# Fused attention and MLP on one core: scores and products in 64x32 tiles

## The chip, the core and the metric

The kernel runs on one core of a Trainium2 chip. A core has engines with a queue each: TensorE (PE; its weight loads are listed as PEld), VectorE (DVE), ScalarE (ACT), GpSimd (POOL) and SyncE (SP), which here only issues DMAs. Each engine takes its instructions in order; they wait for each other by semaphores. The metric is device microseconds (us) of one execution. Three runs of the kernel before took 413.98, 414.71 and 415.77 us.

## The reference

```python
def reference(A_x, A_wqkv, A_wo, B_x, B_w1, B_b1, B_w2, B_b2):
    # _A_ref: x @ wqkv -> 16 heads of 28; softmax(q k^T * 28**-0.5) v; @ wo
    # _B_ref: gelu(x @ w1 + b1, tanh form) @ w2 + b2
    x = A_x                                  # 1 x 2048 x 448, bfloat16
    xn = _layernorm(x, axis=-1)
    s = _A_ref(xn, A_wqkv, A_wo)
    g = _silu(_B_ref(xn, B_w1, B_b1, B_w2, B_b2))   # hidden width 1792
    return x + s * g
```

So there is a softmax over 16 heads x 2048 x 2048 scores, an MLP with 448 x 1792 and 1792 x 448 weights, and projections of 448 x 448.

## The kernel before

*Tiling.* A head's 28 elements are padded to 32, so that four heads fill 128 partitions: four head groups g. The queries are cut into four chunks c of 512. A block b = 4g + c holds the work of one head group on one chunk: 16 tiles of 128 keys x 4 heads, 64 score tiles m of 128 keys x 512 queries, each one PSUM bank. There are 16 blocks and 1024 score tiles. (In the last block, the tiles are cut to 256 and then to 128 queries, so that the end can begin earlier.) The eight PSUM banks are one pool, `ring`, which all matmuls share.

*The chain for a score tile.* TensorE writes the scores into a bank (`t_score`, L1731). Then either ScalarE takes the exponential of two or three neighbouring banks in one instruction (`p_exps`, L1785), or VectorE makes an approximate exponential of one bank by integer arithmetic (`p_apass`, L2065) for tiles set apart ("late", by fours, one for each head, `p_late`); for the late tiles, VectorE (L2138) or POOL (L2132) then writes two shifted copies, which are multiplied with scaled values `vs`. TensorE multiplies the results with the values (`t_pv`, L2320) and adds up over the keys in one accumulator bank per block. A 1 in the padded values gives the softmax denominators too.

*The other products.* Projections q, k, v, the hidden layer (`p_f1`), the second layer (`p_f2`) and the output projection (`p_out`) go through `_mm` (L128), in the same queue between the scores. Gelu of the hidden layer is done at one stretch on ScalarE (L1620), since it needs another function table; tanh for silu comes in four instructions (L1657, L1692). Block b ends in `p_epi`: VectorE copies the accumulator (L2404) or adds it to a partial sum kept in SBUF (L2210, L2212, L2402), the denominators go by DMA through DRAM and POOL's power (L2416) and return as `rb`, and POOL multiplies (L2427) into the place of the block's queries. An output tile of 128 rows needs the four blocks of its chunk; `t_oev` multiplies it with the gate and adds x, by ScalarE's copy and VectorE (L2454, L2456, L2465, L2479) where all exponentials are out, by VectorE (L2458) otherwise.

*Tile shapes of TensorE.* A matmul can use a part of the 128 x 128 array, given as rows x columns. Three shapes are used: 128x128 at the start, 128x32 for all products (four side by side, one for each 32 columns of the output), 32x128 for scores (each head's 32 rows; up to four heads side by side, each into its own bank). `four` lets a score task take four banks; `rest`/`finish` split the last, half empty k tile of a product into two 32x128 matmuls that join a score task; `p_pad` and `p_alone` put one head's queries into `qpad`, zeros for the other heads, so that a single late score tile can run in shape 128x32.

*Order of the work.* The order of all instructions is fixed at build time by a planner (`run`). It keeps a modelled time for each engine, and takes the task that can start first, weighted by priorities and due marks (`planned`). `start_of` gives a task's start: in its terms a change of shape costs `SWITCH` and scores of different heads overlap. `put` issues the task with the waits that it needs. `BP` is a table of constants for each block (`tune`); `NQ` gives the number of late quads in each block, `BN` bursts with partial sums.

Of the kernel before, what the change touches and what calls it, by code (L numbers as in the profile page):

```python
# [16 lines left out]
DH = 28  # L17
F = 1792
G = 4
# [6 lines left out]
NP = 18  # L26
# [4 lines left out]
BPN = ('S4', 'QF', 'MG', 'GQ', 'GE', 'EPS', 'HP', 'JIT', 'RM', 'RG', 'WT', 'PV0', 'PVC', 'MP', 'ND4', 'LU', 'JOINT', 'LQ', 'JMAX', 'DQ', 'URG', 'SLACK', 'UR', 'QLEAD', 'QDIST', 'R3', 'CN', 'CS', 'SR', 'PS', 'PQ', 'BN', 'PVB')  # L31
BP = (
# [17 lines left out]
)  # L50
NQ = (14, 4, 4, 4, 7, 14, 7, 16, 8, 15, 5, 9, 6, 8, 12, 8)
# [45 lines left out]
SEM, OWN, SEMW = 0.07, 0.03, 0.15  # L97
SWITCH = 0.1
# [16 lines left out]
class _Buf:  # L115
    __slots__ = ("w", "r", "tw", "tr")

    def __init__(self):
        self.w = None
        self.r = []  # L120
        self.tw = None
        self.tr = 0.0


def _mm(eng, out, w, x, start, stop):
    ins = None
    for q in range(0, 128, 32):
        ins = eng.matmul(out[q:q + 32, :], w[:, q:q + 32], x, tile_position=(0, q), start=start, stop=stop, skip_group_check=True)  # L128
    return ins


class _Task:
# [6 lines left out]
    def __init__(self, E, fn, reads=(), writes=(), dur=0.1, lat=0.05, prio=5, w=1.0, mode="col", rows=(), port=False, tx=False):  # L139
        self.E, self.fn, self.reads, self.writes = E, fn, list(reads), list(writes)  # L140
        self.dur, self.lat, self.rank, self.w = dur, lat, prio, w
        self.mode, self.rows, self.port, self.tx = mode, set(rows), port, tx
        if E == DVE:
            ov = min(OVERLAP, 0.4 * self.dur)
            self.dur, self.lat = self.dur - ov, self.lat + ov


class _Kernel:
    def __init__(self, nc, A_x, A_wqkv, A_wo, B_w1, B_b1, B_w2, B_b2, out):
# [11 lines left out]
        self.rest_toks = {}  # L161
# [10 lines left out]
        self.run_toks = set()  # L172
# [34 lines left out]
    def start_of(self, t):  # L207
        s = self.tE[t.E]
        if t.E == PE and t.mode != self.pe_mode:
            s += SWITCH  # L210
        elif t.E == PE and t.mode == "row" and not (t.rows & self.pe_rows):
            s = self.pe_start + 0.01
# [9 lines left out]
        for b in t.writes:  # L222
            mine = b.w is not None and b.w[0] is own
            if not (t.E == PE and mine):
                s = max(s, (b.tw or 0.0) + (OWN if mine else SEM))
            s = max(s, b.tr + (SEMW if t.mode == "row" and t.E == PE else SEM))
        return s

    def put(self, t, start=None):
        if start is None:  # L230
            start = self.start_of(t)
        self.deps(t.E, t.reads, t.writes)
        if t.port and t.E == POOL and start < self.port[POOL] + 4.0:
            self.wait(POOL, self.port_h)
# [8 lines left out]
        if t.E == PE and t.mode == "row":  # L243
            for b in map(id, t.writes):
                if self.rest_toks.get(b) is not None:
                    self.wait(PE, self.rest_toks.pop(b))
                elif b in self.rest_toks:
                    self.rest_toks[b] = (sem, self.evcnt[PE])
        self.prog[t.E].append(lambda eng, f=t.fn, s=sem: f(eng).then_inc(s, by))
        h = (sem, self.evcnt[key])  # L250
        if t.E == PE:
            if t.mode == self.pe_mode == "row" and not (t.rows & self.pe_rows):
                self.pe_rows |= t.rows
            else:
                self.pe_rows = set(t.rows)
            sw = SWITCH if t.mode != self.pe_mode else 0.0
            if t.mode != self.pe_mode:
                self.run_toks = set()
            self.run_toks |= set(map(id, t.writes))
            self.pe_mode, self.pe_start = t.mode, start  # L260
            self.pe_hist.append((start - sw, start + t.dur * t.w))
# [4 lines left out]
        self.tE[t.E] = max(self.tE[t.E], start + t.dur)  # L266
# [6 lines left out]
        if self.after and t.E == PE and t.mode == "row":  # L273
# [89 lines left out]
    def choose(self):  # L363
# [7 lines left out]
        b = self.next_m // 64  # L371
        if self.four(at):
            return True
# [12 lines left out]
        return True  # L386

    def four(self, at):
        p, t, m = self.pend, self.pend["task"], self.next_m
        if not S4 or len(at) < 4 or len(p["ms"]) < 2 or not 64 <= m < MTOT - 2 or self.gu is None and m >= GM - 6 or self.in_gelu():  # L390
            return False
        n = m + 1
        while n in self.late:
            n += 1
        if n >= MTOT or {self.pieces(x)[1] for x in p["ms"]} & {self.pieces(m)[1], self.pieces(n)[1]}:
            return False
        lim = self.start_of(t)
        if lim is None or not self.can(m, lim) or not self.can(n, lim) or QF and self.lq and self.can(self.lq[0][0], lim):
            return False
        lim += JOINT  # L400
        if S4 > 2:
            lim = max(lim, p["due"]() - RM)
        fr = {i: f for i, f in at.items() if f <= lim}
        if len(fr) < 4 or len(fr) - 4 - self.over() < (1, 0, 1, 0, -9)[S4 - 1]:
            return False
        two = [x + y for x in self.runs(fr, 2) for y in self.runs(fr, 2) if x[1] < y[0]]
        if not two:
            return False
        t.writes = [self.b_ring[i] for i in min(two, key=lambda y: max(fr[i] for i in y))]
        return True  # L410
# [23 lines left out]
    def run(self):  # L434
        idle = 0
        while True:
# [5 lines left out]
            for p in self.procs:  # L442
# [11 lines left out]
                elif x[0] == "banks" and x[1]():  # L454
                    ids = self.first(self.idle(), p[3][3])
                    if ids:
                        t = _Task(PE, None, (), [self.b_ring[i] for i in ids], 0.216, 0.17, p[3][2])
                        cand.append((self.start_of(t), p, t))
                elif p[3][0] == "bank" and free is not None and p[5]() and p[3][1]():
                    t = _Task(PE, None, (), [self.banks[free][1]], 0.216, 0.17, *p[3][2:])  # L460
# [19 lines left out]
            if E == PE and t.prio >= UR:  # L480
                sc = [c for c in cand if c[2].E == PE and c[2].prio == 1 and c[2].mode == "row"]
# [2089 lines left out]
```

## Time and profile before

| | |
|---|---|
| runs | 413.98, 414.71, 415.77 us (median 414.71) |
| span of the profiled execution | 412.4 us (its first to its last instruction) |
| mean granted TensorE clock | 1.000 |
| TensorE busy | 395.3 us, 6157 matmuls |
| TensorE weight loads | 144.0 us, 6157 |
| ScalarE busy | 400.7 us, 409 instructions |
| VectorE busy | 345.6 us, 596 |
| POOL busy | 194.7 us, 221 |

The profile has no time of its own around the span; the runs' median is 2.3 us above the span. Busy time counts the pipelined overlap of neighbours on an engine, so the distance between starts tells more about an engine's load than the sum of its durations. In the timeline's lines stand the start, the time of the group, engine, line, operation, output and input by the program's names, sizes, the count, and in brackets the idle time before and what ended it. `xnT`, `h`, `w`, `x_sb`, `kT`, `vaug` appear as targets of exponentials, because their space is used again once they have been read.

### The profile page before, as it was taken

The page shows a single profiled execution, that of the slowest core. Times are in us where ns is not written, and L with a number is a line of the kernel's source. Part 1 is how long each engine was busy: PE and PEld are TensorE (multiplying, and loading weights), DVE is VectorE, ACT ScalarE, POOL GpSimd, SP SyncE. Part 2 cuts the span into 40 slices and gives each one's busy share as a digit, 9 for nine tenths or more (in the row PEclk, how much of TensorE's full clock was granted, in tenths as well). Part 3 has the DMA queues.
Part 4 walks back from the last instruction along what each step waited for, and adds up shares of the span by engine and source line. Part 5 has one row for each costly group of instructions (what it writes and reads, how often), then busy time and mean ns, then how long its engine had stood idle before and what let it go on. Part 6 is the DMA issues. An engine that isn't in the chain of part 4 may idle for free.

```text
span 412.4 us, 14687 instructions
## 1 busy us (share of the span) xinstructions
PE 395.3 (96%) x6157; PEld 144.0 (35%) x6157; DVE 345.6 (84%) x596; ACT 400.7 (97%) x409; POOL 194.7 (47%) x221
## 2 busy tenths in 40 slices
PE   6999999999999999999999999999999999999996
PEld 5543232333322233232224443332332223333453
DVE  8958798896679888989898117999998999899976
ACT  6999999999999999999999999999999999999995
POOL 7494656649982563255632411156157014553040
PEclk9999999999999999999999999999999999999999
DMA  8801110001000000100330000220010003200072
GB/s 254 288 4 42 4 31 2 23 12 30 18 3 30 2 28 8 33 2 2 99 105 18 28 3 7 53 54 12 21 24 10 27 8 58 72 3 29 24 140 94
DMA packets 18784, 17.56 MB, mean 43 GB/s; under 512 B 8941, under 2 KB 15421, under 8 KB 18686
## 3 DMA queue, kind: packets, MB, share of 16 engines
q1 hardware_dynamic: 16734, 13.55, 11.1%
q0 software_dynamic: 1008, 2.49, 3.5%
q8 instruction: 49, 0.80, 0.8%
q10 hardware_dynamic: 976, 0.57, 0.5%
q14 instruction: 17, 0.14, 0.1%
HBM read 12.54 MB, written 2.88 MB: 37 GB/s over the span
## 4 chain that ended last, share of the span: by engine, by line
PE 65%; ACT 20%; issue 8%; DVE 5%; POOL 1%; ACTq 0%; DVEq 0%; POOLq 0%
PE ring L128 31%; PE ring L1731 17%; PE ring L2320 14%; ACT P L1785 12%; ACT h L1785 7%; ACT xnT L1785 2%; PE ring L1293 1%; PE ring L1544 1%; DVE x_sb L2065 1%; DVE st L1036 1%; PE ring L1142 1%; DVE h L2065 0%; PE ring L1109 0%; PE ring L1224 0%; POOL h L1095 0%
## 5 line engine op out<-in xcount | busy, mean ns | idle before, releaser
L1785 ACT ACTIVATE P<-ring 128x1024 bf16<-128x1024 f32 (+1 forms) x236 | 249.3, 1162 | 1.1 <-PE ring L2320 0.3
L1731 PE MATMUL ring<-qT,kT 32*128 32x512 bf16 (+2 forms) x1131 | 130.5, 359 | 5.3 <-ACT P L1785 1.6
L1785 ACT ACTIVATE h<-ring 128x1024 bf16<-128x1024 f32 (+1 forms) x79 | 85.8, 1177 | 0.4 <-PE ring L2320 0.3
L1731 PEld LDWEIGHTS ring<-qT,kT 32*128 32x128 bf16 x1131 | 35.6, 91 | 119.9 <-ACT P L1785 60.2
L2065 DVE TENSOR_SCALAR vaug<-ring 128x512 uint16<-128x512 f32 x92 | 61.0, 683 | 5.9 <-PE ring L1731 3.8
L128 PE MATMUL ring<-xnT,w 128*32 128x512 bf16 x864 | 57.6, 381 | 0.4 <-ACT h L1785 0.2
L128 PE MATMUL ring<-w,h 128*32 128x448 bf16 x896 | 55.5, 355 | 0.2 <-DVE x_sb L2065 0.2
L2320 PE MATMUL ring<-P,vaug 128*32 128x512 bf16 (+2 forms) x606 | 53.7, 351 | 0.8 <-ACT xnT L1785 0.7
L2427 POOL TENSOR_TENSOR qT<-x_sb,E_sb 128x512 bf16<-128x512 f32 x15 | 17.7, 1179 | 67.3 <-PE ring L1731 19.0
L2416 POOL TENSOR_TENSOR rc<-rs,mone 128x16 f32<-128x16 bf16 x11 | 32.7, 2971 | 29.5 <-DMA rs<-E_sb 27.9
L1785 ACT ACTIVATE xnT<-ring 128x1024 bf16<-128x1024 f32 (+1 forms) x39 | 43.1, 1132 | 0.6 <-PE ring L1731 0.6
L2065 DVE TENSOR_SCALAR w<-ring 128x512 uint16<-128x512 f32 x52 | 34.6, 685 | 2.7 <-PE ring L1731 2.1
L128 PEld LDWEIGHTS ring<-xnT,w 128*32 128x32 bf16 x864 | 20.3, 96 | 26.3 <-issue 6.1
L128 PEld LDWEIGHTS ring<-w,h 128*32 128x32 bf16 x896 | 17.9, 95 | 22.8 <-issue 14.0
L2320 PE MATMUL ring<-h,vaug 128*32 128x512 bf16 x201 | 23.4, 383 | 0.4 <-ACT P L1785 0.4
L1435 DVE CAST qT<-ring 128x512 bf16<-128x512 f32 x15 | 10.3, 688 | 15.3 <-PE ring L128 15.0
L2065 DVE TENSOR_SCALAR h<-ring 128x512 uint16<-128x512 f32 x28 | 18.7, 684 | 3.8 <-PE ring L1731 3.6
L2320 PEld LDWEIGHTS ring<-P,vaug 128*32 128x32 bf16 x606 | 15.9, 95 | 15.5 <-issue 7.2
L1558 DVE CAST h<-ring 128x512 bf16<-128x512 f32 x24 | 16.4, 687 | 5.0 <-PE ring L128 4.9
L2065 DVE TENSOR_SCALAR x_sb<-ring 128x512 uint16<-128x512 f32 x28 | 18.5, 682 | 2.5 <-PE ring L1731 1.6
L1441 POOL TENSOR_TENSOR qsq<-qT 128x512 bf16<-128x512 bf16 x12 | 12.5, 1039 | 15.5 <-DVE qT L1435 15.5
L128 PE MATMUL ring<-wv,xnT 128*32 128x112 bf16 (+1 forms) x512 | 18.1, 261 | 0.5 <-issue 0.3
(248 smaller groups left out, 644.0 us busy)
## 6 DMA issues: line engine op xcount, KB each, us to landing
x_sb<-recs SPq DMA_DIRECT2D x60, 64.0 KB, 2.0
w<-in_B_w_dram SPq DMA_DIRECT2D x1, 1568.0 KB, 7.5
w<-in_B_w_dram SPq DMA_DIRECT2D x1, 1344.0 KB, 8.3
x_sb<-in_A_x_dram SPq DMA_DIRECT2D x2, 448.0 KB, 6.8
out_dram<-in_A_x_dram SPq DMA_DIRECT2D x2, 448.0 KB, 10.6
out_dram<-h POOLq DMA_DIRECT2D x4, 224.0 KB, 5.9
out_dram<-h SPq DMA_DIRECT2D x7, 112.0 KB, 2.7
xnT<-wq POOLq DMA_DIRECT2D x1, 512.0 KB, 5.4
```

Of the source, the lines that this page charges most:

```text
L128: ins = eng.matmul(out[q:q + 32, :], w[:, q:q + 32], x, tile_position=(0, q), start=start, stop=stop, skip_group_check=True)
L1036: yield _Task(DVE, lambda eng, i=i, t=t: eng.bn_stats(K.st6[:, i, :], K.x_sb[:, c, t, :]), [K.b_x1t if i == 4 else K.b_x[c] if c else K.b_ ...
L1142: return eng.matmul(bank, w[sl, 3, g * 128:(g + 1) * 128], K.xnT[sl, 3, c * 512:(c + 1) * 512], tile_position=pos, start=False, stop=True, ...
L1435: yield _Task(DVE, lambda eng: eng.tensor_copy(qb, bank), [tok], [qr], 0.7, 0.0, dp)
L1441: yield _Task(POOL, lambda eng: eng.tensor_tensor(qs, qb, qb, ALU.mult), [qr], [tq], 1.1, 0.05, 2, port=True)
L1558: yield _Task(DVE, lambda eng: eng.tensor_copy(dst, bank), [tok], wr, 0.69, 0.0, 2)
L1731: return eng.matmul(dst, K.kT[32 * j:32 * j + 32, g, t * 128:(t + 1) * 128], K.qT[32 * j:32 * j + 32, g, c * 512 + q0:c * 512 + q0 + nq], ...
L1785: return eng.activation(reg[:, i0:i0 + n, :], src, ACTF.Exp, scale=SM_SCALE)
L2065: yield _Task(DVE, lambda eng: eng.tensor_scalar(K.part(u, k).bitcast(dt.uint16), K.like(u, bank), SM_SCALE * LOG2E * 128.0, (127.0 - EXP_ ...
L2320: return eng.matmul(acc[32 * j:32 * j + 32, q0:q0 + nq], w, ap[:, col:col + nq] if len(ap.shape) == 2 else ap[:, col // 128:(col + nq) // ...
L2416: yield _Task(POOL, lambda eng: eng.tensor_tensor(K.rc[:, :], K.rs[:, :], K.mone[:, 0:1].to_broadcast([128, 16]), ALU.pow), [K.b_srs, K.b_ ...
L2427: yield _Task(POOL, lambda eng: eng.tensor_tensor(dst, K.rb, E, ALU.mult), [K.b_rb, tE], [K.b_onT[g][c]], 1.15, 0.05, 1, port=True)
```

## The change

Block 0 and the last block stay in the shapes of before. From the point where the padded queries of block 0 have landed, to the end of block 14, scores and products are matmuls of 64x32: four columns of tiles and two halves of rows, h = 0 and 1.

- *Scores* (`t_half`). A half's 64 rows hold two heads. `qp` holds the queries of one head in 32 of the 64 rows and zeros in the other 32, so the matmul over 64 rows gives one head's scores. There are two such arrangements (v) and two buffers (blocks by turns). `p_strips` fills them by four DMAs on SP for each block, 60 in all, ahead of the block; POOL clears them once (two memsets). `JM` changes the order of the heads, so that neighbouring score tiles are on different halves. A tile needs four matmuls of 64x32 for its four key strips.
- *Products* (`product`, `t_pv`). Each k tile of 128 is run as two halves, first all k tiles on one half, then on the other. Both add to the same bank. Where a bank goes from one half to the other with nothing read between, `put` adds a wait of TensorE on its own semaphore ("turn"). The empty half of the last k tile is left out. Two products may be under way at once (`PW`).
- *Planner.* It keeps a time for each half (`tH`), and a constant each for issue, step and turn.
- *Removed*: `rest`, `finish`, `four`, `p_alone`, `qpad`. `P` has 16 slots in place of 18; `qst` shares a buffer of `qsq`.
- *New order.* The table `BP` has other columns and values. `BN` is 0 in all rows, so there are no partial sums in SBUF. In the new program ScalarE has 357 exponentials of two banks, 19 of three and 1 of one (before 286 and 68); 252 score tiles are late (before 248); of the shifted copies, VectorE makes 80 and POOL 92 (before 92 and 64). TensorE has 12,221 matmuls, 10,680 of them 64x32; changes of shape fall from 643 to 111; waits of TensorE on itself rise from 14 to 201. The third chunk's four output tiles come after the last exponential (before, one of them).

```diff
-def _mm(eng, out, w, x, start, stop):
+def _mm(eng, out, w, x, start, stop, h=None):
     ins = None
+    r0 = 64 * (h or 0)
+    if h is not None:
+        w, x = w[r0:r0 + 64, :], x[r0:r0 + 64, :]
     for q in range(0, 128, 32):
-        ins = eng.matmul(out[q:q + 32, :], w[:, q:q + 32], x, tile_position=(0, q), start=start, stop=stop, skip_group_check=True)
+        ins = eng.matmul(out[q:q + 32, :], w[:, q:q + 32], x, tile_position=(r0, q), start=start, stop=stop, skip_group_check=True)
     return ins
...
+SEMX, GAP, STEP = 0.12, 0.016, 0.216
+HB0, HB1 = 0, 15
+TURN = 0.4
+JM = (0, 2, 1, 3)
...
+        if t.E == PE:
+            for b in t.writes:
+                if t.mode == "half" and b.ph is not None and b.ph != t.rows:
+                    self.wait(PE, b.w)
+                b.ph = t.rows if t.mode == "half" else None
+        else:
+            for b in t.reads:
+                b.ph = None
...
+    def half(self, m=None):
+        b = min(self.next_m if m is None else m, MTOT - 1) // 64
+        return HB0 <= b < HB1 and self.pad_b.get(b, 1e9) <= self.now
...
+    def product(self, tok, f, ks, rd, dur, prio):
...
+        h, first = K.side(), True
+        for h in (h, 1 - h):
+            K.on[h] += 1
+            for k in ks[h]:
+                yield _Task(PE, lambda eng, k=k, h=h, s=first: f(eng, k, h, s), rd, [tok], dur, 0.17, prio, mode="half", rows=h)
+                first = False
+            K.on[h] -= 1
+        return True
...
+    def t_half(self, m, bank, tok, prio):
+        K = self
+        b, j, pc, _, _ = K.pieces(m)
+        g, h, v = b // C, j // 2, j % 2
+        sl = slice(64 * h, 64 * h + 64)
+
+        def f(eng):
+            ins = None
+            for t, q0, nq, col in pc:
+                for q in range(0, 128, 32):
+                    ins = eng.matmul(bank[q:q + 32, col:col + nq], K.kT[sl, g, t * 128 + q:t * 128 + q + 32], K.qp[sl, b % 2, v, q0:q0 + nq],
+                                     tile_position=(64 * h, q), start=True, stop=True, skip_group_check=True)
+            return ins
+        return _Task(PE, f, K.score_reads(m), [tok], STEP, 0.17, prio, mode="half", rows=h)
...
+    def p_strips(self):
+        K = self
+        for b in range(HB0, HB1):
...
+                for k in (v, v + 2):
+                    sl = slice(32 * k, 32 * k + 32)
...
+                    h = K.dma(SP, lambda eng, sl=sl, v=v, q=q, i=b % 2: eng.dma_start(K.qp[sl, i, v, :], q), K.s_pad[b % 2][v],
+                              reads=[K.b_qT[g][c]], writes=[] if k > v else [tok], land=land)
...
         if own:
-            if (c, t) in XADD:
+            if (c, t) in XADD and not K.flushed:
```

More of the change, by code (lines that the diff above doesn't have):

```diff
@@ L205, in mark, with start_of @@
             b.tr = max(b.tr, end)
[L207 to L212, printed above, removed]
+    def start_of(self, t, own=True):
+        s = self.tE[t.E] if own else 0.0
+        if t.E == PE and own:
+            if t.mode != self.pe_mode:
+                s = max(self.tH) + SWITCH
+            elif t.mode == "half":
+                s = max(self.pe_issue, self.tH[t.rows])
+            elif t.mode == "row" and not (t.rows & self.pe_rows):
+                s = self.pe_start + 0.01
+            else:
+                s = max(self.tH)
         if t.port:
@@ L225, in start_of @@
                 s = max(s, (b.tw or 0.0) + (OWN if mine else SEM))
+            elif t.mode == "half" and b.ph is not None and b.ph != t.rows:
+                s = max(s, b.tw + SEMX)
             s = max(s, b.tr + (SEMW if t.mode == "row" and t.E == PE else SEM))
@@ L272, in put @@
         self.log.append((start, t))
-        if self.after and t.E == PE and t.mode == "row":
+        if self.after and t.E == PE and t.mode in ("row", "half"):
             self.after[0] += 1
@@ L385, in choose @@
             t.writes = [self.b_ring[i] for i in tri]
[L386 to L409, printed above, removed]
         return True
@@ L1301, in filler @@
             acc, tok = self.accb
+            h = None if not self.half() else self.side() if tok.ph is None else tok.ph
             def f(eng):
@@ L1588, in p_direct @@
             K.dir_b.append(ids)
[L1589 to L1591 removed]
+            two = K.half() and nf == 2
+            for turn, k, n in [(x, k, n) for x in range(2) for k in range(KT) for n in range(nf)] if two else [(0, k, n) for n in range(nf) for k in range(KT)]:
+                yield K.t_f1((f0 + n) // FT, (f0 + n) % FT, K.ring[:, ids[n], :], K.b_ring[ids[n]], k, 3.5,
+                             n ^ turn if two else None, k == turn == 0)
             K.dir_n += 1
@@ L1942, in p_pad @@
         K = self
-        yield _Task(POOL, lambda eng: eng.memset(K.qpad[:, :], 0.0), [], [K.b_pad], 1.1, 0.05, 2)
+        yield ("until", lambda: K.ln_done >= 2 * C and K.boot())
+        for i in range(2):
+            yield _Task(POOL, lambda eng, i=i: eng.memset(K.qp[:, i, :, :], 0.0), [], K.b_pad[i], 2.2, 0.05, 2)
+            if not i:
+                K.spawn(K.p_strips(), 0)
         def f(eng):
@@ L1989, in can @@
         g, c = b // C, b % C
-        return all(x.tw is not None and x.tw + SEM <= st + JOINT for x in [self.b_qT[g][c]] + [self.b_kT[g][p[0] // 4] for p in pc])
+        q = self.b_pad[b % 2] if self.half(m0) else [self.b_qT[g][c]]
+        return all(x.tw is not None and x.tw + SEM <= st + JOINT for x in q + [self.b_kT[g][p[0] // 4] for p in pc])
     def near(self, st):
```

370 lines of the change are left out of this document (175 added, 195 removed), and 33 rows, old and new, of the table BP.

## Prediction

> **What bounds the kernel now.** I read the page first (busy shares), then the busy time of each engine by stretch, then the groups of instructions by form for ScalarE, then ScalarE's and TensorE's timelines for the distance between neighbours.
>
> ```profile
> span 412.4 us, 14687 instructions
> PE 395.3 (96%) x6157; PEld 144.0 (35%) x6157; DVE 345.6 (84%) x596; ACT 400.7 (97%) x409; POOL 194.7 (47%) x221
> ```
>
> ```profile
> 12.96:224.13 211.17, 204.36 (x2985) 68.36 (x2977) 178.57 (x297) 210.49 (x211) 122.46 (x135) 1.00 0.12 34
> 224.13:252.56 28.43, 27.66 (x506) 13.21 (x502) 9.76 (x16) 28.39 (x27) 7.74 (x5) 1.00 0.04 12
> 252.56:406.17 153.61, 151.45 (x2515) 54.28 (x2507) 142.81 (x236) 152.10 (x148) 53.00 (x48) 1.00 0.18 40
> 406.17:412.40 6.23, 2.54 (x68) 1.23 (x60) 3.47 (x8) 1.68 (x4) 1.03 (x1) 0.99 0.23 76
> ```
>
> Columns of the second fence: stretch, its length, then busy us of PE, PEld, DVE, ACT, POOL. The stretches are exponentials, gelu, exponentials, tail. ScalarE is busy without a break from its first exponential (12.96) to its last tanh (406.17), 393.21 us, with TensorE close behind. Busy time includes overlap, so I take the distance between neighbours' starts instead:
>
> ```profile
> 12.96 8.64 ACT L1785 ACTIVATE P<-ring 128x1024 bf16<-128x1024 f32 x9
> ...
> 100.33 1.99 ACT L1785 ACTIVATE h<-ring 128x1024 bf16<-128x1024 f32 x2
> 102.14 1.10 ACT L1785 ACTIVATE P<-ring 128x1024 bf16<-128x1024 f32 x1
> ...
> 194.27 1.49 ACT L1785 ACTIVATE h<-ring 128x1536 bf16<-128x1536 f32 x1
> 195.60 1.50 ACT L1785 ACTIVATE P<-ring 128x1536 bf16<-128x1536 f32 x1
> ...
> 271.48 1.69 ACT L1657 ACTIVATE w<-w 128x1792 bf16<-128x1792 bf16 x1
> 273.07 3.91 ACT L1785 ACTIVATE P<-ring 128x1024 bf16<-128x1024 f32 x4
> ...
> 406.17 0.59 ACT L1692 ACTIVATE w<-w 128x448 bf16<-128x448 bf16 x1
> ```
>
> ```profile
> L1785 ACT ACTIVATE P<-ring 128x1024 bf16<-128x1024 f32 x190 | 188.1, 1076 | 0.7 <-PE ring L2320 0.3
> L1785 ACT ACTIVATE P<-ring 128x1536 bf16<-128x1536 f32 x46 | 69.7, 1516 | 0.4 <-PE ring L1731 0.2
> L1785 ACT ACTIVATE h<-ring 128x1024 bf16<-128x1024 f32 x64 | 65.8, 1096 | 0.4 <-PE ring L2320 0.3
> L1785 ACT ACTIVATE xnT<-ring 128x1024 bf16<-128x1024 f32 x32 | 32.8, 1052 | 0.6 <-PE ring L1731 0.6
> L1785 ACT ACTIVATE h<-ring 128x1536 bf16<-128x1536 f32 x15 | 22.8, 1523 | 0.0
> L1785 ACT ACTIVATE xnT<-ring 128x1536 bf16<-128x1536 f32 x7 | 10.5, 1497 | 0.0
> ```
>
> A two-bank exponential costs (102.14 − 100.33)/2 = 0.905 us, a three-bank one 1.33, a large tanh 1.59. With 190 + 64 + 32 = 286 and 46 + 15 + 7 = 68 of them: 286 × 0.905 + 68 × 1.33 = 258.8 + 90.4 = 349.2 us. Add gelu, 28.4, and the tanh stage, 6.0 (three large, a fourth of three quarters the size taken at 1.2). That is 383.6 of 393.2, so only 9.6 us are gaps in which ScalarE waits for a bank. No change that leaves ScalarE's work as it is can gain more than these 9.6 us and the ends.
>
> TensorE is what makes most gaps:
>
> ```profile
> 154.69 0.39 PE L2320 MATMUL ring<-h,vs 128*32 128x512 bf16 x4
> 155.01 0.40 PE L1731 MATMUL ring<-qT,kT 32*128 32x512 bf16 x4
> 155.34 0.40 PE L1463 MATMUL ring<-qsq,bsel 128*32 128x512 bf16 x4
> 155.56 0.39 PE L2320 MATMUL ring<-w,vs 128*32 128x512 bf16 x4
> ...
> 158.73 0.40 PE L1731 MATMUL ring<-qT,kT 32*128 32x512 bf16 x4
> 159.17 0.69 DVE L2065 TENSOR_SCALAR vaug<-ring 128x512 uint16<-128x512 f32 x1 [0.23 <-PE ring L1731]
> ```
>
> ```profile
> L1731 PE MATMUL ring<-qT,kT 32*128 32x512 bf16 x939 | 121.9, 384 | 5.2 <-ACT P L1785 1.6 <-ACT h L1785 0.9 <-DVE wv L2212 0.2
> L128 PE MATMUL ring<-xnT,w 128*32 128x512 bf16 x864 | 57.6, 381 | 0.4 <-ACT h L1785 0.2 <-DVE w L2065 0.2
> ```
>
> Groups of the same tile shape stand 0.22 us apart (155.34 to 155.56), groups of different shape 0.32 and 0.33: a change of shape costs 0.11 us. By this price, all rows of the groups by form, of which the two above are the largest: 4,836 matmuls of 128x32, scaled by columns, are 1,046 groups of four at 0.215, 224.9 us; 313 groups of 32x128 scores, 67; full-size ones, 8; and 643 changes of shape in the program's order, 70.7. That is 371 of 393 us: 22 us of slack, and the queue is in order.
>
> **The change, part by part.**
>
> *ScalarE and VectorE's share of the scores.* In the order of the new program, ScalarE has 357 two-bank, 19 three-bank and one one-bank exponentials (0.48 by the two distances above): 323.1 + 25.3 + 0.5 = 348.9, against 349.2. Four score tiles more go to VectorE. Gain 0.3 us. Three-bank exponentials were cheaper per bank (0.443 against 0.453); that loss is in the sum.
>
> *Tile shape.* 10,680 matmuls of 64x32 stand in for most of the 128x32 and 32x128 ones, 2,670 groups of four, 1,370 on the upper and 1,300 on the lower half of the rows. If the two halves run side by side as the row tiles of the scores do in the trace, a pair takes 0.215 us; scaled by columns, 275 us. What stays 128x32 is 37, full size 8, scores of block 0 and the last block 9. Changes of shape fall from 643 to 111, 12 us. Sum 341 us: slack 52 us where it was 22. Scores with zeros stream twice the array they did before; that is inside the 275.
>
> *Number of instructions.* PE has 12,221 matmuls for 6,157. The dispatch must keep up: eight loads and matmuls in 0.215 us, 27 ns each.
>
> ```profile
> 391.50 0.23 PEld L1731 LDWEIGHTS ring<-qT,kT 32*128 32x128 bf16 x16 [0.21 <-ACT P L1785]
> ...
> q8 instruction: 49, 0.80, 0.8%
> ```
>
> Sixteen loads in 0.23 us, 14 ns each: half of what is needed, so I charge nothing; the cover is the streaming of 512 columns. The Trainium skill speaks against it: "TensorE: Matmul & The Clock Gate", section "Wait — 56ns, not 53.3ns?", says that starts of matmuls never come closer than about 25 ns. By it a pair of half groups could not take less than 0.200 us, which binds the pairs of 448 and 336 columns (226 and 56 of them, at 0.187 and 0.143 without it): 226 × 13 + 56 × 57 ns = 6.1 us of TensorE, and 0.5 us of the sum below. The row above, at 14 ns, does not agree. The program's own fetches (q8: 49 for the whole kernel) about double for PE; at 0.8% of the DMA time I charge nothing.
>
> *Turn waits.* Where one half adds to a bank after the other, the new kernel makes PE wait on its own semaphore: such waits go from 14 to 201. No row shows one. The bound below is nothing (another group lies between); above, a group is out after 0.40 us (its busy time; VectorE started 0.44 after it), less the 0.22 that the half would be busy anyway: 0.18 × 201 = 36 us. The whole queue stands behind a wait: next scores, thus ScalarE. In the order of the new program 158 of 201 wait for a group three or more groups back. At 0.11 us a group, one three back has 0.07 to go, two back 0.18, one back 0.29: with 53, 27 and 14 of these and two at zero distance, 3.7 + 4.9 + 4.1 + 0.8 = 13.5 us. I take 13.5 at the most and 0 at the least, 36 for the range.
>
> *VectorE and POOL.* Partial sums of the products with P go:
>
> ```profile
> L2212 DVE COPY wv<-ring 128x512 f32<-128x512 f32 x12 | 8.2, 684 | 1.3 <-PE ring L2320 1.2
> L2402 DVE TENSOR_TENSOR E_sb<-ring,wv 128x512 bf16<-128x512 f32 x12 | 8.2, 683 | 0.1
> L2132 POOL TENSOR_TENSOR x_sb<-w,shc 128x512 int32<-128x512 int32 x12 | 12.2, 1037 | 3.8 <-DVE w L2138 2.0 <-DVE x_sb L2138 1.0 <-DVE h L2138 0.7
> 158.91 0.55 SPq L1959 DMA_DIRECT2D qpad<-qT  x1
> ```
>
> 16.4 us less on VectorE, 8 less for twelve shifts that go, 8.2 more for twelve plain copies of the sums, and 2.7 for four more late tiles: about 14 us net, at 84% busy. It frees banks earlier; I count it as nothing by itself, but take the gaps nearer the low end for it. POOL gets 28 shifts × 1.04 = 29 us, 47% to 54%. It is not the bound, but its queue delays the multiplication that ends each block.
>
> *SP and the padded queries.* Sixty small DMAs, four for a block, less 13: each takes some 0.55 us on SP's queue, 33 us over 400, and they are issued a block ahead, about 26 us, so they are hidden. If they were late, the block would begin in the old shape; price: its share of shape changes.
>
> *The tail.* Before, block 14's multiplication is done at 395 and only one of the third chunk's output tiles is left behind the last exponential:
>
> ```profile
> 393.85 1.16 POOL L2427 TENSOR_TENSOR qT<-x_sb,E_sb 128x512 bf16<-128x512 f32 x1 [16.43 <-PE ring L1731]
> ...
> 406.81 0.96 PE L128 MATMUL ring<-wo,qT 128*32 128x448 bf16 x16
> 407.57 0.40 PE L128 MATMUL ring<-h,ident 128*32 128x448 bf16 x4
> 407.81 0.54 ACT L2454 ACTIVATE h<-ring 128x448 bf16<-128x448 f32 x1 [1.05 <-PE ring L128]
> 408.48 0.39 DVE L2456 TENSOR_TENSOR h<-h 128x448 bf16<-128x448 bf16 x1
> ```
>
> In the new order this multiplication is one of the last two on POOL, behind shifts, and all four tiles of that chunk (64 matmuls, four ScalarE copies, eight VectorE additions) stand behind the last exponential. Three more tiles cost 3 × 0.76 = 2.3 on PE (406.81 to 407.57) or 3 × 2 × 0.39 = 2.3 on VectorE, beside each other, and one copy of 0.54 more in the chain: 2.8, range 2.3 to 3.5. The stretch after tanh grows from 6.2 to 9.0.
>
> *The sum.* 12.96 + 348.9 + 28.4 + 6.0 + 9.0 = 405.3, plus the gaps. These I scale by the inverse of TensorE's slack. With turn waits at nothing: 9.6 × 22/52 = 4.1. At 13.5 us: slack 39, 9.6 × 22/39 = 5.4. I take 4.5, for VectorE's relief: span 409.8. The profiled execution of before has 412.4 where the median of runs is 414.71, 2.3 us more; with the same added, 412.1.
>
> **The rivals.**
>
> *Turn waits and same-half runs take the slack* (the other side). The 201 waits cost near their upper price, because the groups that stand between are themselves on the half that is blocked. At 36 us TensorE has 16 us of slack, gaps 9.6 × 22/16 = 13.2, time 405.3 + 13.2 + 2.3 = 420.8; halfway, 418. No change is reached with gaps of 7.1: slack 30, so 22 us for 201 waits, 0.11 us each. For it: the in-order queue, and 2,670 groups fall in 2,164 runs on one half. Against: a median distance of three to four groups. The Trainium skill ("TensorEngine Tiling (Array Packing)", "Gotcha 1: PSUM Pressure") says that different row tiles cannot access one PSUM bank at the same time and software must synchronize. That is why the waits can't be dropped; no run here shows what happens without them.
>
> *Gaps do not depend on TensorE's slack.* They come from when banks are read. The waits view has 149 waits of score loads for a ScalarE read, in total 60.2 us:
>
> ```profile
> PEld ring L1731 <- ACT P L1785: 60.2, 149, 0.8
> ```
>
> That is 0.40 each, what a change of shape and the drain of the group ahead explain already, so I do not read it as idle TensorE. If it is, gaps stay at 7 to 9.6 and the longer tail eats the rest: 414.6 to 417.2, middle 415.7.
>
> *Nearly all gaps close* (0 to 2): 407.6 to 409.6.
>
> *Dispatch is the limit.* If a load with its matmul takes 30 ns with both halves in use, and not 14, a pair of groups takes 0.24 instead of 0.215: 1,335 × 0.025 = 33 us more of TensorE, slack 19, gaps 9.6 × 22/19 = 11, time 418.7. It decides from 27 ns on. The row of sixteen loads speaks against it; it shows the smaller number only for one burst.
>
> *The halves do not run side by side* (the change doesn't do what it says): 2,670 × 0.21 = 560 us of TensorE, over 560. Four row tiles and four column tiles do run side by side in the trace, so it is unlikely.
>
> **How the numbers follow.** About 0.5% (2 us) is what a measurement of this kernel can tell from no change; the runs of before alone span 1.8 us. Gaps shrink as forecast: 0.42, 412.1, own range 409 to 412.6. Nearly all close: 0.04. Gaps as before: 0.25, of it 0.20 within 0.5% and 0.05 slower. Turn waits: 0.22. Dispatch: 0.04. Not side by side, or another loss: 0.03. Faster 0.46, same 0.20, slower 0.34. The range 408 to 420.5 leaves out the top of the turn waits and the last case, about 0.10, and the bottom of the full closure.
>
> **What would show it.** Right: pairs of half groups 0.11 us apart on average in TensorE's timeline; ScalarE's gaps (from first exponential to last tanh less the same sum) about 4.5 us, tanh at about 401; 9 us after it with four output tiles; VectorE below 82%, POOL above 50%. Wrong: PE's loads waiting for PE itself with 0.2 us or more in total over 20 us (turn waits); eight loads in more than 0.22 us everywhere (dispatch); PE idle for 0.5 us and more with ScalarE waiting, at equal distances (program fetches); SP's strips landing after the block's first score; or a tail of other length than 9 us.

## The result, and the profile after

The changed kernel takes 429.15 us (median of 426.67 to 430.14), the kernel before 414.42 beside it: 1.034 times as long, 95% interval 1.031 to 1.038. The forecast was 412.1 us in a range of 408 to 420.5. The profiled execution has 428.93 us, 2.2 over its span of 426.7.

The page of the changed kernel: busy times, the queue of program fetches (q8: packets, MB, share of the DMA engines' time), and the chain of work that ended last. Under it is the same chain line of the kernel before:

```profile
span 426.7 us, 27054 instructions
PE 408.6 (96%) x12221; PEld 208.1 (49%) x12221; DVE 331.0 (78%) x568; ACT 403.8 (95%) x435; POOL 224.8 (53%) x250
...
q8 instruction: 95, 1.56, 1.5%
...
PE 86%; ACT 6%; issue 4%; DVE 2%; POOL 1%; ACTq 0%; POOLq 0%; DVEq 0%
```

```profile
PE 65%; ACT 20%; issue 8%; DVE 5%; POOL 1%; ACTq 0%; DVEq 0%; POOLq 0%
```

Busy time by stretch, with the columns as in the prediction (exponentials, gelu, exponentials, tail):

```profile
12.88:228.16 215.28, 209.17 (x6064) 97.34 (x6060) 176.61 (x291) 211.69 (x227) 120.06 (x132) 1.00 0.15 40
228.16:259.05 30.89, 29.35 (x1017) 16.48 (x1004) 13.06 (x19) 29.06 (x27) 15.58 (x14) 1.00 0.26 52
259.05:417.66 158.61, 155.82 (x4946) 84.92 (x4934) 124.86 (x202) 151.66 (x157) 77.63 (x72) 1.00 0.15 34
417.66:426.70 9.04, 4.98 (x124) 2.68 (x116) 5.59 (x15) 3.33 (x7) 1.03 (x1) 0.94 0.53 140
```

The granted clock is 1.00 up to the tail, so it does not explain the gaps ahead of it. VectorE is down and POOL up as said. In the chain that ended last, TensorE's share rises from 65% to 86% and ScalarE's falls from 20% to 6%. ScalarE now waits for 0.8 to 1.7 us at a time (its timeline; the bracket is the idle time ahead and what ended it):

```profile
92.50 2.85 ACT L1790 ACTIVATE P<-ring 128x1024 bf16<-128x1024 f32 x3 [0.93 <-PE ring L1734]
...
236.39 1.02 ACT L1603 ACTIVATE h<-ring 128x1024 bf16<-128x1024 f32 x1 [0.89 <-PE ring L136]
...
275.48 3.77 ACT L1790 ACTIVATE P<-ring 128x1024 bf16<-128x1024 f32 x4 [1.72 <-PE ring L136]
...
280.06 1.94 ACT L1790 ACTIVATE P<-ring 128x1024 bf16<-128x1024 f32 x2 [0.81 <-PE ring L2341]
```

Split as in the prediction (exponentials by their distances, gelu and tanh stages, tail after the last tanh's start; the rest are gaps of ScalarE), in us of the profiled spans. For the kernel before, exponentials and gaps come out within 0.2 us of the prediction's sum. The last four columns are the gaps by place: ahead of 40 us, from there to gelu, the 115 us behind gelu, and the last 30 to 45 us:

| kernel | span | first exp. | exponentials | gelu | tanh | gaps | tail | <40 | to gelu | behind | last |
|---|---|---|---|---|---|---|---|---|---|---|---|
| before | 412.4 | 13.0 | 349.0 | 28.4 | 6.0 | 9.8 | 6.2 | 0.7 | 4.0 | 3.7 | 1.4 |
| changed | 426.7 | 12.9 | 348.5 | 30.9 | 6.0 | 19.4 | 9.1 | 1.3 | 6.8 | 7.3 | 4.1 |

So of 14.3 us, gaps bring 9.6, the tail 2.9, gelu 2.5; the exponentials give 0.5 back.

What TensorE does in the gaps stands in its own timeline. The bracket "issue" is time in which it waits for nothing that the profile shows:

```profile
216.21 0.39 PE L2341 MATMUL ring<-P,vaug 64*32 64x512 bf16 x4
217.63 0.40 PE L136 MATMUL ring<-xnT,wq 64*32 64x512 bf16 x4 [1.04 <-issue]
...
272.97 0.38 PE L1734 MATMUL ring<-qp,kT 64*32 64x512 bf16 x1
273.95 0.41 PE L1734 MATMUL ring<-qp,kT 64*32 64x512 bf16 x7 [0.61 <-issue]
```

The second pair is the plainest: a group of matmuls of one score tile stops after its first matmul, where the program has no wait, and goes on 0.98 us later. Yet the halves do run side by side: here two groups start 0.02 us apart, the next two 0.2 us later, and each takes 0.39:

```profile
119.93 0.39 PE L2341 MATMUL ring<-w,vaug 64*32 64x512 bf16 x4
119.95 0.39 PE L1734 MATMUL ring<-qp,kT 64*32 64x512 bf16 x4
120.15 0.39 PE L2341 MATMUL ring<-x_sb,vs 64*32 64x512 bf16 x4
120.16 0.39 PE L136 MATMUL ring<-xnT,wq 64*32 64x512 bf16 x4
```

### The profile page after: what moved, and what is told of

Same layout as the page of the kernel before. It is cut to its first block, busy times and chain, and to the rows that moved or that the text cites. A ratio compares the mean times of both kernels' runs of the same rounds, so it can differ in the third digit from the quotient of the medians.

```text
span 426.7 us, 27054 instructions
## 1 busy us (share of the span) xinstructions
PE 408.6 (96%) x12221; PEld 208.1 (49%) x12221; DVE 331.0 (78%) x568; ACT 403.8 (95%) x435; POOL 224.8 (53%) x250
## 4 chain that ended last, share of the span: by engine, by line
PE 86%; ACT 6%; issue 4%; DVE 2%; POOL 1%; ACTq 0%; POOLq 0%; DVEq 0%
PE ring L136 31%; PE ring L1734 25%; PE ring L2341 23%; ACT P L1790 5%; PE ring L1711 3%; PE ring L1517 2%; PE ring L1307 1%; ACT h L1790 1%; POOL x_sb L2142 0%; ACT xnT L1790 0%; PE ring L1238 0%; DVE h L2500 0%; PE ring L1259 0%; DVE h L2477 0%; DVE qT L1294 0%
## 5 line engine op out<-in xcount | busy, mean ns | idle before, releaser
L1734 PE MATMUL ring<-qp,kT 64*32 64x512 bf16 x3460 | 200.7, 381 | 2.3 <-issue 0.9
L1734 PEld LDWEIGHTS ring<-qp,kT 64*32 64x32 bf16 x3460 | 59.0, 89 | 87.8 <-ACT P L1790 35.2
L136 PE MATMUL ring<-w,h 64*32 64x448 bf16 (+1 forms) x1736 | 99.0, 350 | 0.0
L2341 PE MATMUL ring<-P,vaug 64*32 64x512 bf16 (+3 forms) x971 | 93.3, 361 | 1.1 <-PE ring L1734 0.7
L136 PE MATMUL ring<-xnT,w 64*32 64x512 bf16 x1664 | 88.4, 377 | 1.5 <-issue 1.4
L136 PEld LDWEIGHTS ring<-w,h 64*32 64x32 bf16 (+1 forms) x1736 | 41.9, 92 | 16.2 <-issue 1.8
L1790 ACT ACTIVATE xnT<-ring 128x1024 bf16<-128x1024 f32 (+2 forms) x44 | 45.5, 1088 | 1.7 <-PE ring L2341 1.0
L2341 PE MATMUL ring<-h,vaug 64*32 64x512 bf16 (+2 forms) x405 | 44.7, 376 | 0.2
L136 PEld LDWEIGHTS ring<-xnT,w 64*32 64x32 bf16 x1664 | 33.4, 91 | 21.4 <-PE ring L136 3.9
L2341 PEld LDWEIGHTS ring<-P,vaug 64*32 64x32 bf16 (+1 forms) x971 | 28.0, 92 | 10.9 <-issue 1.6
L136 PE MATMUL ring<-xnT,wq 64*32 64x512 bf16 (+1 forms) x372 | 30.4, 379 | 1.2 <-issue 1.0
```

The lines of the kernel that those rows point to most:

```text
L1734: ins = eng.matmul(bank[q:q + 32, col:col + nq], K.kT[sl, g, t * 128 + q:t * 128 + q + 32], K.qp[sl, b % 2, v, q0:q0 + nq], tile_position= ...
L1790: return eng.activation(reg[:, i0:i0 + n, :], src, ACTF.Exp, scale=SM_SCALE)
L2341: return eng.matmul(acc[32 * j:32 * j + 32, q0:q0 + nq], w[sl], ap[sl, col:col + nq] if len(ap.shape) == 2 else ap[sl, col // 128:(col + n ...
```

## The experiments

Three theories: A, TensorE's own program arrives too slowly, now that it has twice the instructions; B, the queue in order and runs of groups on one half; C, the turn waits. The decisive runs keep the changed kernel's order on every engine and alter only what one task of TensorE issues.

**Half the count (e1).** Each group of four 64x32 matmuls becomes two of 64x64:

```diff
-    for q in range(0, 128, 32):
-        ins = eng.matmul(out[q:q + 32, :], w[:, q:q + 32], x, tile_position=(r0, q), ...)
+    n = 32 if h is None else 64
+    for q in range(0, 128, n):
+        ins = eng.matmul(out[q:q + n, :], w[:, q:q + n], x, tile_position=(r0, q), ...)
# and likewise in the scores, the values' projection and the products with P
```

> The changed kernel with every 64x32 group of four matmuls issued as two matmuls of 64x64: same order on all engines, same streaming time, same waits, but 6,893 matmuls in place of 12,221 (the products with P read two of the four heads, so the output is not the reference's). Theory A (TensorE's own program, fetched 16 KB at a time, arrives late: stalls of about 1 us without a semaphore): fetches fall from 95 to about 54, the long stalls mostly go, 416 to 421 us. Theory B (the in-order queue: runs on one half and waits for ScalarE and VectorE hold both halves): nothing changes, 427 to 430. Theory C (turn waits): the same as B.

Measured 423.25 us (423.14 to 423.53), 1.019 times before (1.016 to 1.023), 5.9 us less than the changed kernel, with 54 fetches. Gaps 13.5, gelu 30.4. This has theory A's sign, but the gain is smaller than its range of 416 to 421 asks for; B and C foresaw no change.

**Less streaming, same count (e2).**

```diff
     for q in range(0, 128, 32):
+        if h is not None and not start:
+            c = x.shape[-1] // 2
+            ins = eng.matmul(out[q:q + 32, :c], w[:, q:q + 32], x[:, :c], tile_position=(r0, q), ...)
+            continue
# and likewise in the products with P
```

> The changed kernel with every accumulating 64x32 matmul behind the first of its bank cut to half its columns (half of the sums is left out): same order, same number of instructions, same waits, about 40% less streaming. Theory B: TensorE has room, ScalarE's gaps fall to 1 to 4 us and the time to 409 to 413. Theory A: 95 fetches and their stalls of about 1 us stay, 417 to 423. Theory C: the waits stay but groups land sooner, 420 to 426.

Measured 429.13 us (427.27 to 429.57): no change at all, though TensorE's array has far less to do. That lies above the ranges of all three theories, A's too, but B, which asked for the largest gain, falls as the main cause. TensorE's timeline in the gelu stage of this run shows stops in the middle of groups, waiting for nothing:

```profile
241.89 0.51 PE L138 MATMUL ring<-xnT,w 64*32 64x256 bf16 x24
...
242.49 0.34 PE L138 MATMUL ring<-xnT,w 64*32 64x256 bf16 x7
243.87 0.40 PE L138 MATMUL ring<-xnT,w 64*32 64x256 bf16 x13 [1.03 <-issue]
...
245.76 0.56 PE L138 MATMUL ring<-xnT,w 64*32 64x256 bf16 x23
247.59 0.28 PE L138 MATMUL ring<-xnT,w 64*32 64x256 bf16 x1 [1.27 <-issue]
```

Where in the program are these stops? I numbered the matmuls of the trace, took the distances over 0.7 us between neighbours' starts from 227 us to 282, and set them beside the starts of the q8 packets of 16 KB:

```
e2_narrow: matmul, its number mod 128, stop at us, length, us from the last fetch's start to the end of the stop
6206  62  227.89  1.16  2.36
6334  62  232.14  0.82  2.85
6590  62  239.11  0.75  2.35
6718  62  242.55  1.31  2.39
6846  62  246.05  1.54  2.35
6974  62  250.03  1.02  2.35
7101  61  254.33  0.84  2.23
7229  61  258.21  1.49  2.58
7612  60  271.72  1.24  2.39
7739  59  277.06  1.19  2.44
```

(One stop at 274.33, number 7691, with 4.6 us since its fetch, is left out: it waits for ScalarE. The matmul of the last row has a wait too, but that one had ended 0.7 us earlier.) The stops are whole multiples of 128 matmuls apart, but for a slow drift. A matmul goes with a load of weights: 24,442 instructions in 95 fetches of 16 KB are about 257 a fetch, 128 pairs. Each stop ends 2.2 to 2.9 us after a fetch began, most of them 2.35. And fetches never follow each other closely: the least distance between two of them is 3.54 us in the kernel before, 3.27 in the changed one (median 3.94), 3.35 in this run, 3.33 in e7 below. So TensorE gets at most 128 pairs in about 3.3 us over a longer time, 26 ns a pair. Two full groups side by side, eight pairs in 0.215 us, ask for one in 27; groups of 448 columns for 23, so whatever was lost can hardly be made up. It is no fixed price of each pair: between the stop that ends at 243.87 us and the next, 128 pairs go out in 2.19 us, 17 ns each. Why blocks come no faster is not shown; a fetch itself takes only about 1.1 us (1.5% of 16 DMA engines' time for 95 of them).

**A quarter of the count (e5), and with less streaming besides (e6).** As e1 and e2, with one matmul of 64x128 for a group.

> The changed kernel with every 64x32 group issued as one matmul of 64x128: same order, streaming and waits, 4,229 matmuls (the products with P read one head of four, so the output is not the reference's). Supply theory (TensorE gets its instructions in blocks of 16 KB, 128 pairs of load and matmul, no faster than one block in about 3.3 us): the run with half the count still had gaps of ScalarE of about 13.5 us; if some of these are supply, the time falls below 421. In-order theory for what is left (runs on one half, waits for ScalarE and VectorE): the same as with half the count, 422 to 424.

> The run before with, besides, half the columns in every accumulating matmul behind the first of its bank (half of these sums is left out): few instructions and 40% less streaming. If supply and streaming in order are the two causes and nothing else, ScalarE's gaps fall to 1 to 4 us and the time to 409 to 413. If waits or banks cause the rest, it stays above 416.

Measured e5 421.16 us (421.0 to 421.4), 1.015 times before (1.013 to 1.017); e6 418.25 (418.1 to 418.44), 1.008 (1.006 to 1.010). e5 lies between the two ranges given for it: below 422 to 424, and 0.2 us short of "below 421". e6 misses 409 to 413; it is the other branch, above 416, that came true. The pages of e5 and e6:

```profile
span 419.0 us, 11070 instructions
...
PE 406.4 (97%) x4229; PEld 182.2 (43%) x4229; DVE 327.0 (78%) x568; ACT 401.7 (96%) x435; POOL 224.9 (54%) x250
...
q8 instruction: 33, 0.54, 0.6%
```

```profile
span 415.9 us, 11070 instructions
...
PE 366.3 (88%) x4229; PEld 171.8 (41%) x4229; DVE 327.8 (79%) x568; ACT 400.7 (96%) x435; POOL 224.5 (54%) x250
```

Split as above:

| kernel | span | gelu | gaps | tail | <40 | to gelu | behind | last |
|---|---|---|---|---|---|---|---|---|
| changed | 426.7 | 30.9 | 19.4 | 9.1 | 1.3 | 6.8 | 7.3 | 4.1 |
| e1, half the count | 421.0 | 30.4 | 13.5 | 9.6 | 1.3 | 4.2 | 3.9 | 4.2 |
| e2, less streaming | 426.5 | 29.5 | 20.7 | 9.1 | 1.3 | 6.4 | 8.8 | 4.2 |
| e5, a quarter | 419.0 | 29.5 | 13.1 | 9.1 | 1.3 | 4.0 | 3.6 | 4.2 |
| e6, both | 415.9 | 28.7 | 10.9 | 9.1 | 1.3 | 3.1 | 2.4 | 4.2 |

Supply is worth 8.0 us by the runs (7.7 by the spans: 6.3 of gaps, 1.4 of gelu). With few instructions streaming counts too, but for 2.9 us only. What keeps e6 above the kernel before is not in the middle of the kernel (5.5 us of gaps for 7.7 before) but in the last stretch and the tail, which no edit of these moved.

The stops can be counted over the whole trace, without regard to fetches: all distances over 0.5 us between the starts of neighbouring matmuls with no wait for a semaphore in between.

| kernel | stops | us in all |
|---|---|---|
| before | 0 | 0 |
| changed | 8 | 7.8 |
| e1, half the count | 1 | 1.1 |
| e2, less streaming | 21 | 21.8 |
| e5 and e6, a quarter | 0 | 0 |
| e7, before with 11,532 | 9 | 11.6 |
| e8, before with 8,989 | 4 | 6.2 |

Every one of them ends 2.1 to 3.0 us after a fetch began. The 7.8 us of the changed kernel are about what e5 gains, and six of its eight stops stand at the very matmuls where e2 stops too.

**The kernel before with more instructions (e8, e7).** The other direction: the common helper, and then scores and products with P too, issue a matmul as two of half the columns.

```diff
+    n = N // 2 if N >= 336 else N
+    for s in (slice(i, i + n) for i in range(0, N, n)):
         for q in range(0, 128, 32):
-            ins = eng.matmul(out[q:q + 32, :], w[:, q:q + 32], x, ...)
+            ins = eng.matmul(out[q:q + 32, s], w[:, q:q + 32], x[:, s], ...)
```

> The kernel before in its own order, with only the products that go through the common helper issued in two halves of the columns where they have 336 or more: 8,989 matmuls for 6,157, same sums, same streaming. Supply theory: between before and the run with 11,532, some 3 to 8 us over before, 418 to 423, with long stalls where these products stand close together. In-order theory: 414 to 417.

> The kernel before, in its own order, with each matmul of 336 columns or more in the column and row shapes issued as two of half the columns: same streaming, 11,532 matmuls for 6,157, the result is the reference's. Theory A: fetches go from 49 to about 90, long stalls come as in the changed kernel, 420 to 426 us. Theories B and C: 414 to 417.

Measured e8 421.4 us (419.79 to 422.9), 1.016 times before (1.012 to 1.020); e7 430.48 (429.74 to 432.6), 1.037 (1.033 to 1.041). e8 is in the supply theory's range; e7 is 4.5 us above theory A's. So the kernel before, in its own order and shapes, becomes as slow as the changed one when it has 11,532 matmuls (gaps 25.5 us in its span of 429.4). In both runs a part of the computation is lost, against what is said above: the first term of each split sum in its first half of columns. That the second half's start flag reaches the whole bank explains it, and the size fits: one output tile of 16 (`PADD`) has x as the first term of such a sum, so losing x in half its columns makes a relative error of √(1/32) = 0.177; both outputs are off by 0.178. The Trainium skill ("PSUM — Partial Sum Buffer", "The four PSUM rules") says that the flag clears the marks of a whole bank of 2 KB. The lost terms change no instruction's kind or time. The waits of TensorE's loads on "issue" (us in all, times, longest) in the kernel before, then in e7, where the longest grow from 0.8 and 0.5 us to 2.7 and 1.3, and e7's fetches:

```profile
PEld ring L128 <- issue: 33.3, 141, 0.8
PEld ring L1731 <- issue: 20.5, 56, 0.5
```

```profile
PEld ring L131 <- issue: 38.9, 148, 2.7
PEld ring L1736 <- issue: 30.3, 132, 1.3
```

```profile
q8 instruction: 91, 1.49, 1.5%
```

**64x64 and 64x32 mixed (e1b).** e1 without its edit to the products with P, so that the whole result is computed.

> The changed kernel, whole, with scores and all products but those with P as matmuls of 64x64 (two for a group), those with P in 64x32: 8,165 matmuls, but 1,215 changes of tile shape instead of 111. If a change between 64x64 and 64x32 costs nothing: 422 to 425. If it costs 0.11 us like the change between 128x32 and 32x128 did: 1,100 x 0.11 = 120 us of TensorE, far above 440.

Measured 671.66 to 752.5 us, far above 440. A change between these two shapes costs what the change between 128x32 and 32x128 did: 0.32 us from start to start in its timeline, at a granted clock of 1.00, and over such a change the halves do not overlap. (The granted clock falls to 0.82 in the later part of this run, so its total does not measure the price.)

```profile
200.16 0.40 PE L2343 MATMUL ring<-h,vaug 64*32 64x512 bf16 x4
200.48 0.41 PE L1736 MATMUL ring<-qp,kT 64*64 64x512 bf16 x4
```

So the count cannot be cut in this way without losing more.

**No turn waits (e3), old shapes (e4), fewer late tiles in block 14 (e9).** These alter what the planner sees.

```diff
# e3, in product(); the products with P likewise
-        for h in (h, 1 - h):
+        for x in (h, 1 - h):
...
-            for k in ks[h]:
+            for k in ks[x]:
# e4
-HB0, HB1 = 0, 15
+HB0, HB1 = 0, 0
# e9, row of block 13 in the table: NQ1
-    (..., 4.03, 8, 0.42, 1),
+    (..., 4.03, 4, 0.42, 1),
```

> The changed kernel with both parts of a product on one half (the same 64 rows twice, so half of each sum is left out and half is counted twice), so that no bank changes its half and no turn wait is left (0 for 201); the planner's order is made anew. Theory C: ScalarE's gaps fall by 8 us or more, below 421. Theories A and B: 425 to 432, fetches and in-order blocking are as before.

> The changed kernel with the 64x32 shape switched off for all blocks: everything else of the change stays (constants, no partial sums, no joined tasks), the planner makes the order anew for 128x32 products and 32x128 scores: 7,962 matmuls, 580 changes of shape, ScalarE with 248 two-bank and 96 three-bank exponentials. If the number of instructions through the 64x32 shape is the main loss of the changed kernel: 414 to 421. If the new order without it is worse by itself (constants made for the other shape, the last half k tile back in the products): 425 or more.

> The changed kernel with one constant of the table other (late quads of block 14: 4 for 8), so that the order is the same up to block 13 and POOL has fewer shifted copies ahead of block 14's multiplication: two instead of four of the third chunk's output tiles are behind the last exponential. If the end of the kernel costs as said (2.8 us for three tiles more), the stretch behind the last tanh falls from 9.1 to 7.2 us and the time by 1.5 to 2.5, to 426.5 to 427.7; the gaps ahead of block 13 stay. If the end is set by something else: no change.

Measured e3 471.39 us (470.92 to 473.19), e4 465.37 (461.77 to 466.23), e9 433.56 (432.31 to 437.9). e3 and e9 lie outside all that was said; e4 falls under "425 or more", the new order being worse by itself. e9's tail went from 9.1 to 10.7 us and its gaps from 19.4 to 27.0. The likely reason is that the constants were chosen for another order. As the order changed together with what was to be tested, these runs show nothing of turn waits, the old shapes or the tail.

**A short tail (e10), and with a quarter of the count (e11).** Order kept; three of the third chunk's tiles are cut to 16 columns.

```diff
+            nn = 16 if g and c == C - 2 and t < 3 and h is None else D
-            return _mm(eng, ps, K.qT[...], K.wo[:, g, :], start, g == G - 1, h)
+            return _mm(eng, ps[:, :nn], K.qT[...], K.wo[:, g, :nn], start, g == G - 1, h)
# and likewise the copy, the multiplication and the addition in t_oev
```

> The changed kernel in its own order, with the work of three of the third chunk's four output tiles behind the last exponential cut to 16 of 448 columns (their matmuls behind the first term, ScalarE's copy, the multiplication and the addition; the rest of these tiles is left out). If the longer end costs its 2.8 us through this work: the stretch behind the last tanh falls from 9.1 to 6.2 to 7 us, the time by 2 to 3, and the gaps ahead do not move. If the last instruction fetches or the DMAs set the end: less than 1 us.

> The run with a quarter of the count (421.2) and the short tail together. If the supply of instructions and the end are separate terms that add: 418 to 419.5, 10 us below the changed kernel, and 3 to 5 us over before, which then lie in the gaps of the last 30 us and in gelu. If they share a cause: 420.5 or more.

Measured e10 430.23 us (429.01 to 432.56): no change; tail 8.8 us, not 6.2 to 7. In this tail stands a stop without a wait, of 1.0 us from start to start, that the changed kernel's own tail does not have; it ends 2.4 us after a fetch began:

```profile
421.99 0.56 PE L136 MATMUL ring<-wo,qT 128*32 128x448 bf16 x8 [0.64 <-issue]
```

So e10 may show too little of what the shorter work gains. e11 has no such stop: 420.63 us (420.07 to 420.99), 0.5 us under e5, tail 8.1. That is in the range of "420.5 or more", not because the terms share a cause but because the work of the tail is a small term. The tail of e11:

```profile
412.08 0.29 DVE L2418 TENSOR_TENSOR qT<-ring,w 128x128 bf16<-128x128 f32 x1
...
412.43 1.42 PE L137 MATMUL ring<-wo,qT 128*32 128x448 bf16 x40 [0.82 <-DVE qT L2418]
```

TensorE, with less to do, just waits: behind the first tiles stands the last chunk's last tile, which needs VectorE's reciprocal, and the remaining tiles of the third chunk are queued behind that. By e11 tile work is 1.0 of the 2.9 us. The timeline suggests that the place in the queue is what is left; no run changed that alone.

## Why the prediction was wrong

- *The number of instructions* is the first step that failed: "Sixteen loads in 0.23 us, 14 ns each: half of what is needed, so I charge nothing", and the fetches "at 0.8% of the DMA time I charge nothing". The row showed the rate within a block that had arrived; the rate over blocks is 26 ns a pair (least distance between fetches). The least distance of 25 ns between starts, which the prediction sets against this row, does not show either: a whole block of e2 went out at 17 ns a pair. It is worth 8.0 us of the changed kernel's time, and 15.3 us where the kernel before is given as many instructions. The prediction's own sign of it came out: TensorE idle for 0.5 us and more, in step with the fetches. The rival "Dispatch is the limit" had the right place, but 0.04 of the chance and another mechanism, a fixed price of each pair that counts from 27 ns on. Single pairs go out faster than that; it is whole blocks that come late. The Trainium skill ("Runtime: NRT & Kernel Launch", "Instruction fetch mechanics") says that a program is fetched in blocks of 16 KB and that crossing a block is mostly hidden. The blocks are in the traces; that it is hidden holds for the kernel before (49 fetches, a median of 8.2 us apart, and no stop without a wait), not for this one.
- *Gaps as the inverse of TensorE's slack* is the second step that failed, and it weighs as much. The rule gave 4.5 us. With the supply out of the way (e5), the gaps are 13.1 us; ahead of the last stretch they are 8.9, against 8.4 before. Much less streaming (e6) brings these only to 6.8, though it adds a lot of slack. The rival "Gaps do not depend on TensorE's slack" comes near for this part. What sets these gaps in place of the slack stays open: turn waits and groups that follow each other on one half may hold some of them.
- *Turn waits*: an estimate from the starts of the matmuls, each group set against the earliest that its half and the queue allow, has 54 groups that wait for TensorE's own semaphore late by 7.7 us in all, inside the 0 to 13.5 that I gave. Their share in the time was not isolated (e3).
- *The shape itself* did what it says: the halves overlap. What the 532 changes of shape fewer give back was not measured by itself (e4).
- *ScalarE's work*: 348.9 said, 348.5 measured; tanh 6.0, as said. *Gelu* was taken as unchanged, 28.4; it took 30.9, of which 1.4 is supply and 0.8 streaming by e5 and e6.
- *The tail*: 9.0 said, 9.1 measured, which was luck: I priced the work of three tiles, and by e11 this work is only 1.0 us of the 2.9 added. The rest is probably the order of the queue.
- *The last 30 to 45 us* have gaps of 4.1 us for 1.4, which I did not foresee, and they are the same in e1, e2, e5 and e6. TensorE has products of the second layer left over there (120 matmuls of w and h in the last 30 us, none before). That this is the cause was not shown.
- *Two sums of the rivals* are wrong in themselves. "Halfway, 418" does not follow: 18 us of turn waits leave 34 of slack, gaps of 6.2 and 413.8 us. The middle of 414.6 to 417.2 is 415.9, not 415.7.

Against the kernel before, supply 7.7, tail 2.9 and last stretch 2.7 make 13.3 of the 14.3 us. Against the forecast, the span is 17 us too long: 7.7 are supply, 8.6 are gaps that did not close (13.1 in e5 for 4.5), and 1.1 is gelu without supply; the exponentials give 0.4 back.

## What to carry to other kernels

Count a kernel's instructions against the supply: a price from one short burst is not a rate. When tiles get smaller, the instructions for each unit of streaming grow, and the span divided by the number of TensorE's program fetches (the page's q8) says how near the limit one is: 4.5 us a fetch in the changed kernel, 8.4 before, 3.3 at the least. It is an average, though: e8 has 5.9 and had already lost 6.6 us, with stops in some places only. In a tuned order, edit what a task issues and keep the order: runs with a new order told nothing.

## What was not expected of the hardware

- The program of TensorE came in blocks of 16 KB no faster than one in 3.3 us, whatever the matmuls' width (3.27, 3.35 and 3.33 us at the least in the changed kernel, e2 and e7), and stops of about 1 us stand at places of the program that are multiples of 128 pairs apart.
- A start flag on one half of a bank's columns made the next accumulation in the other half overwrite; this is inferred from the size of the error of e7 and e8 (0.178 for 0.177).
- Between 64x64 and 64x32 tiles groups start 0.32 us apart (e1b), as between 128x32 and 32x128; the two halves do not overlap there.
